# One more resident key-weight slice, a mixer ring of four single slices, and a new instruction order in an attention-and-mixer kernel

## Chip, cores and metric

The kernel runs on one core of one Trainium2 chip. The metric is the device time of one execution in microseconds; three executions of the kernel before gave 3256.13, 3258.33 and 3261.33 us, median 3258.33 us.

## What is computed

The reference applies four layers to 2048 tokens of width 640, attention (A), mixer (B), A, B, each with a residual and a layer norm ahead of it:

```python
x = x + _A_ref(_layernorm(x), A_mem0, A_Wq, A_Wk, A_Wv, A_Wo, A_seg_len)
x = x + _B_ref(_layernorm(x), B_w1, B_w2, B_w3, B_w4)
x = x + _A_ref(_layernorm(x), A_mem0, A_Wq, A_Wk, A_Wv, A_Wo, A_seg_len)
x = x + _B_ref(_layernorm(x), B_w1, B_w2, B_w3, B_w4)
```

Attention goes over 64 segments of 32 tokens, one after another. Each segment sees 8 memory tokens and itself (40 rows, 32 heads of 192), and the attention output of the memory tokens is the memory of the next segment:

```python
for s in range(n_seg):
    h = concatenate([mem, x[s*32:(s+1)*32]])      # 40 x 640
    q, k, v = h @ Wq, h @ Wk, h @ Wv              # 32 heads x 192
    o = (softmax(mask(q @ k.T * scale)) @ v) @ Wo # 40 x 640
    mem, out[s] = o[:8], o[8:]
```

The mixer is `h = gelu(layernorm(x) @ w1)`, a shift of its four channel quarters by -1, +1, -2 and +2 tokens, `x1 = x + h @ w2`, and `x1 + gelu(layernorm(x1) @ w3) @ w4` (w1, w2 640x640, w3 640x1536, w4 1536x640).

## The kernel before

**Steps and lanes.** The two attention layers run together: in step t (0 to 68, `attention_step(t)`) lane 0 works on segment t of the first layer and lane 1 on segment t-5 of the second. Steps 5 to 63 have both lanes, 80 rows; the first five and the last five have one, 40 rows. The two mixers run as one stream too: `chunk(c)` and `chunk_end(c)` work on 64 tokens of each lane (128 rows), one chunk in every two steps, spread between the attention work. Two steps and one chunk make a period of the trace. The last chunk runs by itself at the end.

**Attention in a step.** The 32 heads are 8 groups of 4, in 4 pairs `pr`. For a group TensorE makes keys `psk` and queries `psq` (`keys_queries`, 30 matmuls of 80 columns each, L928), values `psv` for the pair (L984, in tiles of 32 columns of the array), scores `pss` (L1044), the transposed weights `pst` (L1079), the output `pso` (L1096) and its share of the output projection `psy` (L1122, 30 matmuls in two halves). ScalarE copies qT, V, PT and oT out of PSUM (L939, L964, L1087, L1104) and does the exponential (L1063); VectorE copies kT and does the softmax. When the last `psy` of a step is done, VectorE copies the memory rows into `hT` (`fm`, L1149 for two lanes), for which the next step's keys and queries wait, and the token rows into `yTB` (`fy`, L1163 and L1165), for which the mixer's `psx` transposes (L1305) wait. In odd steps `fy` is four copies, in even steps two.

**Chunk.** psx, sum with the loaded residual `xw` (L1310), layer norm, transposes `psv` (L1202), w1 (`psh`, L1409), gelu, w2 (`hs`, L1468), layer norm, w3 (`psh`, L1531), gelu, w4 (`y`, L1577), L1592, a layer norm for the second attention, and `psn` (L1631), whose columns go into `hT` (`fc`, L1639). GpSimd's queue issues the loads of the next chunk: `lnx` (L1263) and four of `xw` (L1285). `psvl` (L1202 too) transposes the 64 rows of `lnx` for the first lane.

**Weights.** wq, wk and wv have five slices of 128 rows for a pair (1536 columns, 384 KB each). `STREAM[kind][pr]` of the five are loaded anew through the ring `wst` of twelve slots (`RING_A`, `load_pair`, L802), the rest stay on chip, and so does all of Wo. Odd steps take the pairs in reverse order, and the pair at the turn is kept, so that a step loads three pairs. The mixer's weights all stream, through the ring `wstB` of `RING_B` slots (`load_b`, L838 to L844). All these loads are issued on SyncE's queue in one order, each when its slot is free.

**The order.** Nothing runs in the order of the Python loops. `Plan.add` records every operation with a cost and its reads and writes; `Plan.place` then picks, engine by engine, the operation that its cost model lets start first, and among those within a few hundredths of a microsecond the one with the smallest rank. The ranks are the table `RANK`, a list for each kind of step and operation, found by a search. `OVER`, `DMA_RATE` and `RATE_ONE` belong to that cost model alone. What is built is a fixed order on each engine.

Of the kernel before, what the change touches and what calls it, by code (L numbers as in the profile page):

```python
# [22 lines left out]
STREAM = {"k": (4, 2, 2, 4), "q": (4, 2, 2, 4), "v": (4, 1, 1, 4)}  # L23
RING_A = 12
RING_B = 3
# [24 lines left out]
OVER = 0.0  # L50
PE_LAT = 0.22
DMA_RATE = 335.0e3
# [9 lines left out]
RATE_ONE = 350.0e3  # L62
# [6 lines left out]
        "apply_ln.f": (60.13, 185.694, 121.216, 72.37,),  # L69
        "chunk.f1": (175.755,),  # L70
        "chunk.f2": (76.908,),
        "chunk.f3": (157.464,),
        "chunk.fe": (133.631,),
        "chunk.fe3": (57.268,),
        "chunk.fel": (-12.647,),
        "chunk.fhr": (260.219,),
        "chunk.fhs": (203.515,),
        "chunk.fk0": (74.518,),
        "chunk.fk1": (194.333,),
        "chunk.fs": (103.426, 110.915,),  # L80
        "chunk.ft": (113.011,),
        "chunk.fw": (65.202, 75.684, 108.832, -50.712, 68.19, 10.815, 60.434, 122.265, 56.172, 161.413, 66.001,
            107.816, 153.37,),
        "chunk.fx": (114.535,),
        "chunk.fx0": (91.411, 111.515,),
        "chunk.fxu": (116.315,),
        "chunk.fz": (93.811,),
        "gelu.f1": (189.103, 112.842, 128.034, 132.117, 44.407, 147.123, 98.279,),
        "gelu.f2": (57.845, 81.849, 107.377, 125.496, 54.573, 170.821, 64.393,),
        "gelu.f3": (117.836, 38.035, 94.857, -4.703, 136.729, -25.232, 93.978,),  # L90
        "gelu.f4": (131.7, 41.437, 170.141, 69.53, 69.266, 116.495, 116.698,),
        "ln_ops.f1": (145.801, 200.678,),
        "ln_ops.f2": (71.886, 106.684,),
        "load_b.fn": (147.751, 23.09, 11.08, 11.355, 89.609, 6.762, 92.508, -1.573, 25.172, 111.488, 53.734,
            83.446, 82.888,),
        "transposes.f": (144.968, 58.96, 214.456,),
    },
    "chunk_end": {
        "apply_ln.f": (211.991,),
        "chunk_end.fc": (-27.709, 120.014, 238.626,),  # L100
        "chunk_end.fs": (74.033, 110.691,),
        "chunk_end.fst": (180.769, 113.382,),
        "chunk_end.ft4": (102.714,),
        "chunk_end.fw": (28.061, 167.286, 30.445, 89.214, 81.834, 168.442,),
        "chunk_loads.f": (195.767, 161.598, 81.116, 106.457, 112.814,),
        "chunk_loads.fz": (93.808,),
        "ln_ops.f1": (-34.553,),
        "ln_ops.f2": (106.46,),
        "load_b.fn": (135.743, 100.041, 78.2, 137.787, 32.979, 148.786,),
    },  # L110
    "first": {
        "attention_step.attend.f1": (148.378, 77.62, 114.96, 182.798, 67.707, 132.292, 117.437, 9.556,),
        "attention_step.attend.f2": (94.114, 45.338, 97.34, 2.921, 39.889, 158.104, 102.968, 120.888,),
        "attention_step.attend.f3": (111.391, 103.267, 58.209, 67.757, 59.663, 202.755, 84.112, 126.69,),
        "attention_step.attend.f4": (60.398, 144.455, 13.144, 68.985, 167.013, 76.809, 77.99, 116.342,),
        "attention_step.attend.f5": (165.673, 98.282, 108.051, -30.162, 100.241, 108.627, 50.844, 33.286,),
        "attention_step.attend.f6": (82.907, 61.972, 169.833, 50.782, 87.105, 1.277, 38.193, 13.451,),
        "attention_step.attend.f7": (57.571, 73.411, 92.596, 149.164, 43.781, 166.64, 114.181, 193.617,),
        "attention_step.attend.fs": (94.666, 40.135, 103.519, 45.088, 93.624, 126.408, 53.08, 100.642,),
        "attention_step.fm": (97.138,),  # L120
        "attention_step.fy": (152.471,),
        "attention_step.keys_queries.fk": (108.26, 63.879, 60.273, 80.616, 125.72, 79.278, 129.38, 120.256,),
        "attention_step.keys_queries.fk2": (73.153, 105.038, 173.824, 72.993, 110.733, 23.631, 43.071, 110.049,
            69.986, 59.459, 28.577, 130.679, 2.806, 21.99, 16.502, 38.137,),
        "attention_step.keys_queries.fn": (114.737, 87.54, 90.747, 134.363, 51.243, 12.969, 113.46, 18.309, 28.745,
            52.697, 18.142, 37.915, 100.944, 59.855, 136.199, 114.18, 5.659, 167.958, 120.015, 126.184, -8.685,
            81.081, 81.602, 179.073, 87.637, 106.4, 41.064, -12.77, -26.244, 87.387, 121.946, 65.385, 94.824,
            70.71, 51.535, 27.115, 114.677, 136.151, 54.568, 202.357, 1.163, 126.959, 46.11, 79.263, 50.203,
            103.218, 100.572, 28.338, 116.712, 119.833, 137.44, 106.323, 40.974, 87.854, 51.428, 27.582, 75.954,
            87.949, 63.925, 144.876, 25.025, 136.202, 11.073, 134.566,),  # L130
        "attention_step.keys_queries.fq": (124.433, 100.638, 54.881, 107.011, 54.88, 102.016, 85.177, 108.598,),
        "attention_step.project.f8": (-74.442, -42.266, 137.911, 68.456, 95.985, -20.623, -3.681, 126.264, 137.783,
            79.153, 124.656, 99.94, 174.748, 132.771, 48.335, -27.114,),
        "attention_step.v_copy.fe": (131.77, 40.6, 126.632, 26.958, 166.274, 137.131, 88.073, 100.927, 57.888,
            78.872, 57.842, 101.781, 163.971, 21.423, 65.236, 108.635,),
        "attention_step.values.fv": (121.916, 134.278, 159.944, 48.99, -37.717, 64.118, 22.938, -51.977,),
        "load_pair.fn": (152.205, 115.609, 58.339, 140.914, 17.015, 111.511, 22.712, 203.377, 25.175, 202.14,
            41.521, 59.495, 52.779, 169.347, 9.285, 112.577, 41.187, -43.215, 79.871, 114.893, 5.785, -25.152,
            70.491, 117.135, 22.224, 40.345, -6.819, 171.235, 20.723, -5.808, 154.45, 146.744, 99.11, 126.651,),
        "res_tile.fn": (-37.803, 60.152, -8.701, 68.506, -2.387, 95.473, 16.955, -87.282, 167.605, 123.352, -17.98,  # L140
            5.54, 86.376, 90.625, 112.221, 91.761, -108.652, 143.475, 62.803, 138.743,),
    },
    "last": {
        "apply_ln.f": (152.793, 163.662, 74.991,),
        "chunk.fc2": (46.568, 157.158,),
        "chunk.fhr": (84.809,),
        "chunk.fs": (125.199, 55.502,),
        "chunk.ft": (134.777,),
        "chunk.fw": (141.993, 98.819, 86.347, -34.206, 180.428, 155.267, 138.674, 27.312, 81.939, 168.933, 109.433,),
        "chunk.fx": (47.573,),  # L150
        "chunk.fxu": (60.041,),
        "chunk.fz0": (255.003,),
        "chunk.halves.fa": (88.067, 111.942, 48.413, 110.73,),
        "chunk.halves.fn": (100.468, 138.108,),
        "gelu.f1": (101.778, 153.798, 120.238, 107.304, 104.078, 95.762,),
        "gelu.f2": (88.059, 54.923, 64.114, 67.676, 143.026, 71.513,),
        "gelu.f3": (147.997, 245.442, 214.387, 69.54, 186.357, 71.876,),
        "gelu.f4": (177.876, 105.904, 39.072, 140.832, 33.224, 81.409,),
        "ln_ops.f1": (61.467, -50.049,),
        "ln_ops.f2": (110.805, 201.056,),  # L160
        "load_b.fn": (97.929, 101.637, 88.373, 99.2, 6.248, -22.885, 93.276, 79.47, 154.946, 116.487, 54.257,
            111.859, 111.308,),
        "transposes.f": (29.26, -72.55,),
        "warm.fwarm": (228.987, 45.787, 114.595, -52.726, 202.36, 124.17, 102.55, 80.655, 222.205, 89.395, 108.587,
            48.077, 96.179,),
    },
    "last_end": {
        "chunk_end.fs": (44.631, 85.191,),
        "chunk_end.fst": (110.886, 86.277, 2.303, 125.225,),
        "chunk_end.fw": (70.696, 6.036, 95.78, 131.599, -11.939, 104.166, 94.79, 51.751,),  # L170
        "load_b.fn": (0.449, 34.393, 103.284, 139.892, 157.41, 27.939,),
    },
    "start": {
        "apply_ln.f": (58.226,),
        "chunk_loads.f": (176.973, 88.206, 110.091,),
        "ln_ops.f1": (88.7,),
        "ln_ops.f2": (121.638,),
        "start.f1": (19.368,),
        "start.f2": (83.017,),
        "start.f3": (89.709,),  # L180
        "start.f4": (41.06,),
        "start.f5": (107.925, -3.163, 55.808, 83.534,),
        "transposes.f": (149.113,),
    },
    "step0": {
# [399 lines left out]
def kernel(  # L585
# [177 lines left out]
    def mm_us(n, m=128, k=1):  # L763
        return k * (max(54, n) / 2400.0 + 0.0025)
# [972 lines left out]
```

## Time and profile before

| | |
|---|---|
| median of three runs | 3258.33 us |
| the profiled execution: time, span | 3268.68 us, 3266.9 us |
| granted TensorE clock, mean | 0.993 |
| TensorE busy | 3149.0 us, 96% |
| VectorE, ScalarE, GpSimd busy | 70%, 57%, 8% |
| bytes moved | 833.44 MB, 255 GB/s |
| mixer loads `wstB` | 495 of 320 KB, 132 of 160 KB |
| attention loads `wst` | 556 keys, 556 queries, 418 values, 384 KB each |

The trace has one row for each instruction of an engine with its start and length, and names what ended an engine's idle time ahead of it. A matmul row runs from its issue to its result, some 0.2 us, while the next one can be issued after some 0.036 us (80 columns), so matmuls overlap in the trace. Therefore a pause of TensorE is best read from the starts of its groups, and the idle time that the trace gives is shorter than the pause.

### The profile page before, as it was taken

Reading aid. Unit: us, or ns where it says so; the run is one execution under the profiler, and the core shown is the slowest. Engines: PE = TensorE matmul, PEld = TensorE weight load, DVE = VectorE, ACT = ScalarE, POOL = GpSimd, SP = SyncE. Lnnn points to the kernel's source line nnn. Section 1 sums busy time; section 2 is a strip of 40 time slices with the busy share of each in tenths; the row PEclk is TensorE's granted clock in tenths of the full one; section 3 lists DMA queues with packets and bytes.
Section 4 is the critical chain, followed back from the end, with each engine's and each line's share of the span. In section 5 each row is a group of like instructions: output and inputs, shape, how many; then the busy total and the mean of one; then the engine's idle time right before and its main releaser. Section 6 shows DMA issues by size and latency. Waiting matters only on the chain.

```text
span 3266.9 us, 172868 instructions
## 1 busy us (share of the span) xinstructions
PE 3149.0 (96%) x77161; PEld 2790.2 (85%) x77161; DVE 2285.5 (70%) x7377; ACT 1854.6 (57%) x4217; POOL 269.6 (8%) x510
## 2 busy tenths in 40 slices
PE   5899999999999999999999999999999999999997
PEld 4778888888888888888888888888888888888875
DVE  3566777777677777777777777777777777767665
ACT  2345565666556666656565666565656665556443
POOL 0000000000000000000000000000000000000000
PEclk8999999999999999999999999999999999999999
DMA  9787777778777877787777777777877787778885
GB/s 372 264 286 236 237 265 253 241 235 273 246 237 249 280 239 234 253 272 239 245 262 258 241 237 269 253 241 244 281 247 238 244 274 249 238 244 277 275 277 199
DMA packets 409714, 833.44 MB, mean 255 GB/s; under 512 B 39651, under 2 KB 207280, under 8 KB 408969
## 3 DMA queue, kind: packets, MB, share of 16 engines
q1 hardware_dynamic: 401704, 809.47, 73.2%
q0 software_dynamic: 7104, 12.84, 1.3%
q8 instruction: 604, 9.90, 1.2%
q14 instruction: 142, 1.16, 0.1%
q10 hardware_dynamic: 160, 0.08, 0.0%
HBM read 816.98 MB, written 5.24 MB: 252 GB/s over the span
## 4 chain that ended last, share of the span: by engine, by line
PE 88%; DMA 7%; issue 2%; DVE 2%; ACT 1%; SPq 0%; POOL 0%; POOLq 0%; ACTq 0%; DVEq 0%
PE psq L928 16%; PE psy L1122 16%; PE psk L928 16%; PE psv L984 15%; PE pss L1044 5%; PE pso L1096 5%; PE psh L1531 3%; DMA wst<-in_A_Wq_dram 3%; PE y L1577 3%; PE pst L1079 2%; DMA wst<-in_A_Wk_dram 2%; PE psv L1024 2%; PE psh L1409 1%; PE hs L1468 1%; DMA wst<-in_A_Wv_dram 1%
## 5 line engine op out<-in xcount | busy, mean ns | idle before, releaser
L928 PEld LDWEIGHTS <-wst 128*128 128x128 bf16 x19872 | 803.7, 99 | 64.1 <-issue 35.7
L1122 PE MATMUL psy<-oT,wo 128*128 128x80 bf16 (+1 forms) x16560 | 703.6, 200 | 26.4 <-issue 8.6
L964 ACT CAST V<-psv 96x384 bf16<-96x384 f32 (+3 forms) x1264 | 595.9, 474 | 168.3 <-PE psv L984 102.4
L1122 PEld LDWEIGHTS <-wo 128*128 128x128 bf16 x16560 | 630.8, 99 | 51.2 <-issue 35.1
L928 PE MATMUL psq<-hT,wst 128*128 128x80 bf16 (+1 forms) x9936 | 518.0, 200 | 13.7 <-DMA wst<-in_A_Wq_dram 8.6
L928 PE MATMUL psk<-hT,wst 128*128 128x80 bf16 (+1 forms) x9936 | 508.6, 200 | 17.7 <-DVE hT L1149 9.6
L939 ACT CAST qT<-psq 128x480 bf16<-128x480 f32 (+1 forms) x552 | 291.8, 529 | 371.2 <-PE psq L928 352.0
L1104 ACT CAST oT<-pso 128x480 bf16<-128x480 f32 (+1 forms) x552 | 293.7, 532 | 264.0 <-PE pso L1096 238.9
L954 DVE CAST kT<-psk 64x160 bf16<-64x160 f32 (+1 forms) x1104 | 340.4, 308 | 131.3 <-PE psk L928 62.6
L984 PEld LDWEIGHTS <-hT 128*32 128x32 bf16 (+1 forms) x11840 | 295.5, 96 | 157.0 <-issue 5.2
L1063 ACT ACTIVATE Pm<-pss,sm 80x320 bf16<-80x320 f32 (+2 forms) x552 | 279.3, 506 | 195.9 <-DVE sm L1056 105.2
L1056 DVE CUSTOM_DVE_ANT_1 pss<-pss,mask 80x320 f32<-80x320 f32 (+2 forms) x552 | 257.1, 466 | 150.1 <-PE pss L1044 138.3
L1087 ACT COPY PT<-pst 80x320 bf16<-80x320 bf16 (+2 forms) x552 | 221.7, 402 | 239.2 <-PE pst L1079 233.3
L984 PE MATMUL psv<-wst,hT 128*32 128x384 bf16 (+1 forms) x5920 | 343.3, 326 | 2.2 <-issue 1.1
L984 PE MATMUL psv<-wv,hT 128*32 128x384 bf16 x5920 | 344.7, 328 | 0.5 <-issue 0.5
L1067 DVE TENSOR_REDUCE sm<-Pm 80x4 f32<-80x320 bf16 (+2 forms) x552 | 250.5, 454 | 109.6 <-ACT Pm L1063 98.1
L928 PE MATMUL psq<-hT,wq 128*128 128x80 bf16 (+1 forms) x6624 | 321.1, 200 | 4.1 <-DMA wq<-in_A_Wq_dram 2.7
L928 PE MATMUL psk<-hT,wk 128*128 128x80 bf16 (+1 forms) x6624 | 321.0, 200 | 3.4 <-issue 2.0
L928 PEld LDWEIGHTS <-wk 128*128 128x128 bf16 x6624 | 270.8, 99 | 17.6 <-issue 13.9
L947 DVE CAST kT<-psk 128x320 bf16<-128x320 f32 (+1 forms) x552 | 253.8, 460 | 45.6 <-PE psk L928 33.5
L1069 DVE TENSOR_TENSOR Pm<-Pm,sm 80x320 bf16<-80x320 bf16 (+2 forms) x552 | 256.2, 464 | 34.9 <-DVE sm L1068 0.9
L928 PEld LDWEIGHTS <-wq 128*128 128x128 bf16 x6624 | 267.4, 99 | 6.5 <-DMA wq<-in_A_Wq_dram 3.0
(131 smaller groups left out, 3777.6 us busy)
## 6 DMA issues: line engine op xcount, KB each, us to landing
wst<-in_A_Wk_dram SPq DMA_DIRECT2D x556, 384.0 KB, 4.9
wst<-in_A_Wq_dram SPq DMA_DIRECT2D x556, 384.0 KB, 5.0
wst<-in_A_Wv_dram SPq DMA_DIRECT2D x418, 384.0 KB, 5.1
wstB<-in_B_w_dram SPq DMA_DIRECT2D x495, 320.0 KB, 4.7
wstB<-in_B_w_dram SPq DMA_DIRECT2D x132, 160.0 KB, 4.3
wo<-in_A_Wo_dram SPq DMA_DIRECT2D x8, 960.0 KB, 12.3
wv<-in_A_Wv_dram SPq DMA_DIRECT2D x2, 1536.0 KB
xw<-in_A_x_dram POOLq DMA_DIRECT2D x32, 77.5 KB, 5.3
```

The costliest lines, as they stand in the source:

```text
L928: nc.tensor.matmul(out=o[:, cc, 0:W], lhsT=wv(kc, GW * j + cc * P, GW * j + (cc + 1) * P), rhs=h[:, kc, cw:cw + W], start=begin(pq), stop= ...
L939: nc.scalar.copy(out=qT[:, :, c0:c0 + N], in_=T(pq)[:, :, off:off + N])
L947: nc.vector.tensor_copy(out=k4[:, :, 0::3, c0:c0 + N], in_=p4[:, :, 0::2, off:off + N])
L954: copy(out=k4[r0:r1, :, jj, c0:c0 + N], in_=p4[r0:r1, :, 1, off:off + N])
L964: (nc.vector.tensor_copy if e == "DVE" else nc.scalar.copy)(out=v_part(*dst), in_=a_)
L984: nc.tensor.matmul(out=o[32 * u:32 * u + n3, :], lhsT=left[:, kc, 32 * g3:32 * g3 + n3], rhs=wv(kc, a, a + GWH), start=(kc == 0), stop=(kc ...
L1056: nc.vector.tensor_tensor_reduce(out=o, in0=o, in1=maskt.unsqueeze(1).to_broadcast([NR, HG, N]), scale=-scale, scalar=3.0e38, op0=ALU.add, ...
L1063: nc.scalar.activation(out=Pb[0:NR, :, 0:N], in_=o, func=ACT.Exp, bias=sm_[0:NR, 0:1], scale=-1.0)
L1067: nc.vector.tensor_reduce(out=sm_[0:NR, 2:2 + HG], in_=Pb[0:NR, :, 0:N], axis=AX.X, op=ALU.add)
L1069: nc.vector.tensor_tensor(out=Pb[0:NR, :, 0:N], in0=Pb[0:NR, :, 0:N], in1=sm_[0:NR, 6:6 + HG].unsqueeze(2).to_broadcast([NR, HG, N]), op=A ...
L1104: nc.scalar.copy(out=o_[:, :, off:off + N], in_=T(pso)[:, :, 0:N])
L1122: nc.tensor.matmul(out=o[:, m, cw:cw + W], lhsT=wo[:, cc, m * P:(m + 1) * P], rhs=o_[:, cc, 0:W], start=st, stop=True, skip_group_check=True)
```

## The change

Pair 1 of the keys keeps four of its five slices on chip instead of three. The mixer's ring becomes four slots of one slice (160 KB) instead of three slots of two (320 KB), so that its w1, w2, w4 and most w3 loads are of one slice and so are the matmul groups that use them; the last columns of w3 keep loads of two slices, which are 256 columns wide there. The last chunk keeps its loads as they were. A new `order` entry holds w1's matmuls behind the `psvl` transposes. The model's three constants are changed, and all of `RANK` is replaced by a new table. No arithmetic is changed, and the number of matmuls on TensorE is the same, 77161.

```diff
-STREAM = {"k": (4, 2, 2, 4), "q": (4, 2, 2, 4), "v": (4, 1, 1, 4)}
+STREAM = {"k": (4, 1, 2, 4), "q": (4, 2, 2, 4), "v": (4, 1, 1, 4)}
-RING_B = 3
+RING_B = 4
-OVER = 0.0
+OVER = 0.03
-DMA_RATE = 335.0e3
+DMA_RATE = 330.0e3
-RATE_ONE = 350.0e3
+RATE_ONE = 345.0e3
 RANK = {
-    ...
+    ...
 }
+    ONES = tuple((k, k + 1) for k in range(KC))
+    PAIRS = ((0, 2), (2, 4), (4, KC))
...
-            b.make = lambda: wring.tile([P, SLOT if last else 2 * Dm], bf16, name="wst" if last else "wstB",
+            b.make = lambda: wring.tile([P, SLOT if last else Dm], bf16, name="wst" if last else "wstB",
...
-            transposes(psl2, vx, TOK, D(0.11), (vxk,))
+            o_l = transposes(psl2, vx, TOK, D(0.11), (vxk,))
...
-        for i, (a, e) in enumerate(((0, 2), (2, 4), (4, KC))):
-            due = D(0.2 + 0.05 * i)
+        for i, (a, e) in enumerate(PAIRS if last else ONES):
+            due = D(0.2 + 0.05 * (a // 2) + 0.01 * (a % 2))
...
-            add("PE", mm_us(128, k=KC * (e - a)), due, fw, r=(wb, vTk, B("vTl"), B("vTd"), B("vTn", 0), B("vTn", 3)), a=tuple(pz))
+            add("PE", mm_us(128, k=KC * (e - a)), due, fw, r=(wb, vTk, B("vTl"), B("vTd"), B("vTn", 0), B("vTn", 3)), a=tuple(pz),
+                order=(o_l,) if ahead else ())
...
-        for i, (a, e) in enumerate(((0, 2), (2, 4), (4, 5))):
+        for i, (a, e) in enumerate(PAIRS if last else ONES):
...
-        for third, (n0, n1, units) in enumerate(((0, 5, ((0, 2), (2, 4), (4, KC))), (5, 10, ((0, 2), (2, 4), (4, KC))),
-                                                 (10, FC, ((0, KC),)))):
+        for third, (n0, n1, units) in enumerate(((0, 5, PAIRS if last else ONES), (5, 10, PAIRS if last else ONES),
+                                                 (10, FC, ((0, KC),) if last else PAIRS))):
...
-        for i in range(6):
-            a, e = 2 * i, 2 * i + 2
-            due = D(1.3 + 0.06 * i)
+        n4 = 2 if last else 1
+        for a in range(0, FC, n4):
+            e = a + n4
+            due = D(1.3 + 0.03 * a)
```

## The prediction

> **What bounds the kernel now.** First the page's busy line and its chain of work that ended last, then the busy time by stretches, which covers the start, the two-lane part and the end.
>
> ```profile
> PE 3149.0 (96%) x77161; PEld 2790.2 (85%) x77161; DVE 2285.5 (70%) x7377; ACT 1854.6 (57%) x4217; POOL 269.6 (8%) x510
> ...
> PE 88%; DMA 7%; issue 2%; DVE 2%; ACT 1%; SPq 0%; POOL 0%; POOLq 0%; ACTq 0%; DVEq 0%
> ```
> ```profile
> 100.00:300.00 200.00, 184.72 (x4822) 158.01 (x4819) 129.12 (x442) 92.94 (x250) 14.13 (x26) 1.00 0.79 268
> 300.00:3000.00 2700.00, 2668.09 (x65194) 2384.74 (x65194) 1961.80 (x6250) 1631.33 (x3615) 228.05 (x424) 1.00 0.75 250
> ```
>
> TensorE is the bound. Of 2700 us with two lanes it idles 31.9, and its 77161 matmuls stay. So the change is worth what it does to TensorE's pauses. TensorE's own waits say what ends them:
>
> ```profile
> PE psk L928 <- DVE hT L1149: 9.6, 29, 0.3
> PE psq L928 <- DMA wst<-in_A_Wq_dram: 8.6, 16, 1.1
> PE psk L928 <- DMA wst<-in_A_Wk_dram: 2.4, 6, 0.8
> ```
>
> The first comes 29 times, once per two steps. Idle time is counted from a matmul's result, 0.2 us after its issue, so pauses are longer than this; I read them from starts. This is the end of an odd step, TensorE and VectorE:
>
> ```profile
> 1525.85 0.31 PE L1079 MATMUL pst<-ident,Pm 80*128 80x80 bf16 x4
> 1526.12 0.70 PE L1122 MATMUL psy<-oT,wo 128*128 128x80 bf16 x15
> 1526.73 0.45 PE L1096 MATMUL pso<-PT,V 80*128 80x80 bf16 x8
> 1527.01 2.05 PE L1122 MATMUL psy<-oT,wo 128*128 128x80 bf16 x45
> 1529.39 0.81 PE L928 MATMUL psk<-hT,wst 128*128 128x80 bf16 x18 [0.33 <-DVE hT L1149]
> ```
> ```profile
> 1529.10 0.24 DVE L1149 CAST hT<-psy 128x80 bf16<-128x80 f32 x1 [3.83 <-PE psy L1122]
> 1529.25 0.33 DVE L1163 CAST yTB<-psy 128x150 bf16<-128x150 f32 x1
> 1529.47 0.17 DVE L1165 CAST yTB<-psy 128x10 bf16<-128x10 f32 x1
> 1529.55 0.32 DVE L1163 CAST yTB<-psy 128x150 bf16<-128x150 f32 x1
> 1529.77 0.17 DVE L1165 CAST yTB<-psy 128x10 bf16<-128x10 f32 x1
> ```
>
> From 1525.85 to 1529.39 are 3.54 us. Issued are 72 matmuls at 0.036 us (the pitch inside such groups), 2.59 us. Paused: 0.95. The last psy issues until about 1528.90 (result at 1529.06, less 0.2, plus its pitch), so 0.49 go to the wait for hT and 0.46 to psy waiting for oT and pso for PT. At an even step's end pst starts at 1575.09 and psk at 1578.70; issued there are 57 matmuls at 0.036 and 25 psh at 0.056, 3.45 us: 0.16 paused. Together 1.11 us in a period of 93.8.
>
> **The change, part by part.** Orders are read from the two built programs; all durations are from the trace.
>
> *Step ends.* From the issue end of pst to its pso the trace needs 0.73 us (1525.99 to 1526.73, with PT's copy of 0.42 between); from pso to its own psy 0.81 (1527.02, oT's copy from 1527.21 for 0.56, then 0.05). Before, 15 psy matmuls (0.54) stood in those places. In the new order 30 do (1.07), at odd and even ends: both waits go, 0.46 + 0.16 = 0.62 us per period.
>
> But at the steps' ends of the two-lane part VectorE now does fy (the yTB copies) ahead of fm (the hT copy), and at odd ends TensorE has psn and psx between the last psy and the first psk. psx needs all of fy. Counted from the last psy's issue: VectorE starts at 0.20; by the starts above the copies follow at 0.22, 0.08 and 0.22, the last takes 0.17, so fy ends at 0.89; psx starts at 0.94 (0.05 from copy to matmul, as 1529.34 to 1529.39) and takes 5 x 0.056 until 1.22. hT, behind fy, is ready at 0.80 + 0.24 + 0.05 = 1.09, earlier. psn (0.15) lies in between; its two copies of 0.29 and 0.17 end near 0.8. So psk starts at 1.22, of which 0.43 is work: a pause of 0.79 against 0.49, 0.30 us more. At even ends hT is ready at 0.20 + 2 x 0.29 + 0.24 + 0.05 = 1.07; the 20 psh matmuls now there hide 1.12 (before, ten hid the 0.49). With that cover gone it would cost up to 1.07 per period, 31 us. Net: 0.62 - 0.30 = 0.32 us gained, times 29 periods: **-9.3 us**.
>
> *psvl.* The five transposes psvl use 64 rows of the array instead of 128, and pauses of 0.1 us set them off on both sides (the pso ahead of them is issued by 1538.98):
>
> ```profile
> 1539.08 0.32 PE L1202 MATMUL psvl<-ident,vbg 64*128 64x64 bf16 x5
> 1539.33 0.82 PE L928 MATMUL psq<-hT,wq 128*128 128x80 bf16 x18
> ```
>
> Five at 0.029 end at 1539.23, psq starts at 1539.33. In the new order the values' psv follow psvl at once, and their own pause ahead of them, of the same size, is paid anyway: 0.1 x 29 = **-2.9 us**. The runs of psv otherwise number much the same (279 and 282).
>
> *The resident slice* takes one 384 KB load out of each step, about 68 x 0.39 = 27 MB, 3% of 833. It can save at most the waits of psq, psk and psv for wst, 8.6 + 2.4 + 0.8 = 11.8 us, and nothing where the slice was hidden anyway. With 0.75 busy DMA engines I take the low end, **-1 us**.
>
> *The ring.* More SyncE issues (35 instead of 19 per chunk, less one k slice a step), no bytes more. Landing times by size:
>
> ```profile
> wstB<-in_B_w_dram SPq DMA_DIRECT2D x495, 320.0 KB, 4.7
> wstB<-in_B_w_dram SPq DMA_DIRECT2D x132, 160.0 KB, 4.3
> ```
>
> The new risk is that a slot must be refilled between its use and the use four units on. Counted in matmul time along the orders, the shortest such distance was 7.6 us with three double slots; now it is 5.1, then 5.2, 5.7, 5.7, 5.9 and 6.1. A refill needs the landing and about 0.3 us from the last matmul's issue to the DMA's. With 4.3 that is 4.6: hidden. With a need of 5.4 it costs 0.3 + 0.2 per period, 15 us. Queued behind such a load on SyncE are the key, query and value slices. Nothing excludes a small gain, since the finer matmul groups can start on half the bytes; its bound is the 1.0 us that y waits for wstB. I take **+2 us**, near the median row; bounds -1 and +15.
>
> A page of the Trainium skill speaks against it. "DMA: Bandwidth & Descriptors", section "Measured (HBM→SBUF, 128 partitions, SWDGE, issued from GpSimd)", says to batch loads to 1 MiB or more, and its section "Anatomy of one DMA" fits a fixed 2 us plus bytes over 436 GB/s. By that fit a 160 KB load would take an estimated 2.4 us and sixteen more loads per chunk 32 us of fixed time if nothing overlapped, 930 us over 29 periods; the rows above, 0.4 us for half the size with loads overlapping, make me expect none of it.
>
> *The chunk's loads.* GpSimd's loads of xw (L1285) wait for the end of w4, which in the new order stands about 7.1 us ahead of the odd end instead of 16.6. After w4, 1.3 us pass until the first issue (L1592 twice, then 0.3), and four issues at 0.55 put the last at -4.15. Landing, by all tiles xw:
>
> ```profile
> DMA to landing us min/median/max: 2.0/4.9/7.1
> ```
>
> At the median it lands at +0.75, and the sum L1310 wants it at 1.22 + 0.24 = 1.46. VectorE is in order: kT copies and the layer norm for psv (L1202) stand behind L1310, the latter with nearly no slack. At the maximum every time it would cost 1.5 x 29 = 43 us. I take **+1 us**.
>
> *Ends of the kernel.* The one-lane steps are reordered too; TensorE idles 15.3 us from 100 to 300. The same covers counted there come out some longer, some shorter: 0, bounds 6 each way (ten steps at 0.6, a two-lane period's gain). The finer matmul groups cost nothing by themselves: inside and between groups the pitch is 0.036.
>
> **Sum.** -9.3 - 2.9 - 1 + 2 + 1 = -10.2 us. The profiled execution took 3268.68 us for a span of 3266.9, 0.3% over the median of 3258.33; so I take the sum off the median: **3248 us**. A measurement can tell 0.2%, 6.5 us, from no change.
>
> **Rivals.** (1) *The ring of four decides* (slower). Place: TensorE at the w3 and w4 units with 5.1 to 5.7 us of distance. Against: y waited only 1.0 us before. For: that was with 7.6 us; now there is 0.5 of slack over the median. If the need is 5.6, it costs 0.5 + 0.4 = 0.9 per period, 26 us: 3274. It outweighs the gain from a need of about 5.35. 0.18. (2) *xw lands late, or fy ahead of hT costs more than counted* (slower): 0.6 us per period more, 17 us: 3265. 0.10. (3) *Given back* elsewhere, by VectorE and ScalarE copies that now come in tighter places: 3255 to 3262. For: 70% VectorE. 0.22. (4) *Weight waits go too*: 10 us more, 3238. Against: 3% fewer bytes. 0.10. That the slice itself does nothing is part of my forecast, which lives on the order.
>
> **Numbers.** The forecast has 0.40, rival 4 0.10: faster 0.50; same 0.22; slower 0.28. The forecast's own range is 3238 to 3252. Below, -10 for weight waits and -6 for the ends with another few: 3226. Above, +15 for the ring, +10 for xw and +6: 3280, which takes in rival 1.
>
> **What would show it.** Right: in the trace after, hT starts about 0.64 us after the odd end's last psy result instead of 0.04, psk starts behind psx, pso and psy stop waiting for PT and oT, and psvl runs into psv. Wrong: waits of psh, hs or y for wstB of several tens of us; VectorE waiting at L1310 for xw; or a pause at even ends behind psh.

## The result and the profile after

The changed kernel took **3285.12 us** (median of six runs, 3270.94 to 3295.52) beside 3259.83 for the kernel before on the same chip: ratio 1.0075, 95% interval 1.0060 to 1.0089. It is slower by 20 to 29 us, under 1%; the forecast was 3248 with a range up to 3280. A second set of five runs gave 3279.84 and 1.0058 (1.0038 to 1.0078).

The executions in the two profiles understate this. Before's took 3268.68, far up in its spread, and after's 3270.94, the lowest of its six. So a second profile of each kernel, from the experiments, stands beside them below. Line numbers of after are those of before plus 4, from about L1410 on plus 5 or 6.

The page of after, busy line and chain of waits that ended last:

```profile
PE 3138.7 (96%) x77159; PEld 2781.0 (85%) x77161; DVE 2271.9 (69%) x7377; ACT 1861.6 (57%) x4217; POOL 267.1 (8%) x510
...
PE 86%; DMA 8%; issue 2%; DVE 2%; ACT 1%; SPq 1%; POOL 0%; DVEq 0%; POOLq 0%; ACTq 0%
```

TensorE is still the bound, with the same matmuls. Its share of the chain has gone from 88 to 86%, and DMA's and SyncE's queue (SPq) from 7 and 0 to 8 and 1. The stretch with two lanes (us, busy time of PE, PEld, DVE, ACT and POOL, clock, DMA share, GB/s):

```profile
300.00:3000.00 2700.00, 2658.48 (x65245) 2376.70 (x65242) 1952.87 (x6254) 1640.67 (x3617) 225.81 (x424) 1.00 0.73 242
```

The clock is at 1.00 as before and the DMA engines are less loaded, 0.73 instead of 0.75, since the resident slice took 27 MB away. TensorE nevertheless idles 41.5 us of these 2700 instead of 31.9. Its waits (us in total, times, longest):

```profile
PE psq L932 <- DMA wst<-in_A_Wq_dram: 20.1, 35, 1.3
PE psx L1309 <- DVE yTB L1169: 19.5, 31, 0.6
...
PE psk L932 <- DVE hT L1158: 1.7, 6, 0.3
```

The wait of psk for hT (9.6 us before) is gone and psx for yTB has come, as worked out. What was not: psq now waits 20.1 us for query slices where it waited 8.6. The end of the odd step that answers to the one shown of before, TensorE and then VectorE:

```profile
1519.93 0.45 PE L1100 MATMUL pso<-PT,V 80*128 80x80 bf16 x8
1520.22 2.32 PE L1126 MATMUL psy<-oT,wo 128*128 128x80 bf16 x60
1522.38 0.31 PE L1637 MATMUL psn<-ident,h2u 128*128 128x64 bf16 x5
1523.33 0.45 PE L1309 MATMUL psx<-ident,yTB 128*128 128x128 bf16 x5 [0.65 <-DVE yTB L1169]
1523.62 0.38 PE L932 MATMUL psk<-hT,wst 128*128 128x80 bf16 x6
```
```profile
1522.58 0.33 DVE L1167 CAST yTB<-psy 128x150 bf16<-128x150 f32 x1 [1.54 <-PE psy L1126]
1522.81 0.17 DVE L1169 CAST yTB<-psy 128x10 bf16<-128x10 f32 x1
1522.88 0.32 DVE L1167 CAST yTB<-psy 128x150 bf16<-128x150 f32 x1
1523.11 0.17 DVE L1169 CAST yTB<-psy 128x10 bf16<-128x10 f32 x1
1523.18 0.23 DVE L1153 CAST hT<-psy 128x80 bf16<-128x80 f32 x1
```

Thirty psy stand behind each pst and none waits. The last psy result is at 1522.54 and hT starts at 1523.18, 0.64 us later, the number of the prediction; psk comes right behind psx.

To see where the time went I added up TensorE's pauses from its starts (distance to the next matmul, less the pitch of its shape; pauses under some 0.06 us are left out) in steps 5 to 63, by what ended each. Columns are profiled executions; us, with the number of pauses. The last row is the time from the first psk of step 5 to the last psy of step 63, between which all five hold the same psk, psq and psy matmuls:

| ended by | before, again | after | after, again | two passed | one passed |
|---|---|---|---|---|---|
| wst (attention slices) | 6.8 x21 | 24.8 x56 | 32.0 x56 | 3.4 x8 | 10.2 x25 |
| wstB (mixer slices) | 0.3 x2 | 1.6 x10 | 1.1 x4 | 27.6 x52 | 2.4 x9 |
| PT and oT | 19.0 x116 | 1.1 x2 | 1.4 x3 | 1.1 x2 | 1.4 x3 |
| hT or psx (step ends) | 14.8 x30 | 23.9 x30 | 23.8 x30 | 23.8 x30 | 23.9 x30 |
| nothing shown, under 0.4 us | 9.6 x77 | 1.4 x8 | 3.1 x17 | 1.8 x9 | 2.1 x10 |
| nothing shown, longer | 10.2 x11 | 6.2 x9 | 4.7 x7 | 12.2 x14 | 10.6 x14 |
| other | 1.3 x6 | 9.9 x61 | 10.1 x62 | 9.6 x61 | 9.9 x62 |
| length of this part | 2773.9 | 2777.5 | 2781.1 | 2785.7 | 2767.6 |

(The last two columns are the runs in which query slices pass mixer loads, below.) The rows of PT and oT and of the step ends did what the sum said. The first row ate it.

### The profile page after: what moved, and what is told of

Read it like the earlier page. It is cut to its first block, busy times and chain, and to the rows that moved or that the text cites. A ratio compares the mean times of both kernels' runs of the same rounds, so it can differ in the third digit from the quotient of the medians.

```text
span 3269.2 us, 173866 instructions
## 1 busy us (share of the span) xinstructions
PE 3138.7 (96%) x77159; PEld 2781.0 (85%) x77161; DVE 2271.9 (69%) x7377; ACT 1861.6 (57%) x4217; POOL 267.1 (8%) x510
## 4 chain that ended last, share of the span: by engine, by line
PE 86%; DMA 8%; issue 2%; DVE 2%; ACT 1%; SPq 1%; POOL 0%; DVEq 0%; POOLq 0%; ACTq 0%
PE psy L1126 16%; PE psk L932 16%; PE psq L932 16%; PE psv L988 15%; DMA wst<-in_A_Wq_dram 6%; PE pso L1100 4%; PE pss L1048 4%; PE psh L1536 3%; PE y L1583 3%; PE pst L1083 2%; PE psv L1028 2%; PE psh L1413 2%; PE hs L1473 1%; PE psv L1206 1%; DMA wst<-in_A_Wk_dram 1%
## 5 line engine op out<-in xcount | busy, mean ns | idle before, releaser
L932 PEld LDWEIGHTS <-wst 128*128 128x128 bf16 x19044 | 777.4, 99 | 77.7 <-issue 37.6
L968 ACT CAST V<-psv 96x384 bf16<-96x384 f32 (+4 forms) x1264 | 589.9, 473 | 299.1 <-PE psv L988 207.2
L1126 PE MATMUL psy<-oT,wo 128*128 128x80 bf16 (+1 forms) x16560 | 692.9, 200 | 16.7 <-DMA wo<-in_A_Wo_dram 7.7
L932 PE MATMUL psq<-hT,wst 128*128 128x80 bf16 (+1 forms) x9936 | 529.9, 200 | 23.5 <-DMA wst<-in_A_Wq_dram 20.1
L932 PE MATMUL psk<-hT,wst 128*128 128x80 bf16 (+1 forms) x9108 | 493.0, 200 | 4.1 <-DVE hT L1158 1.5
L932 PE MATMUL psk<-hT,wk 128*128 128x80 bf16 (+1 forms) x7452 | 349.7, 200 | 3.9 <-issue 2.7
L988 PE MATMUL psv<-wv,hT 128*32 128x384 bf16 (+1 forms) x5920 | 344.8, 328 | 1.2 <-issue 1.1
L932 PEld LDWEIGHTS <-wk 128*128 128x128 bf16 x7452 | 301.0, 99 | 19.3 <-issue 14.6
```

The costliest lines, as they stand in the source:

```text
L932: nc.tensor.matmul(out=o[:, cc, 0:W], lhsT=wv(kc, GW * j + cc * P, GW * j + (cc + 1) * P), rhs=h[:, kc, cw:cw + W], start=begin(pq), stop= ...
L968: (nc.vector.tensor_copy if e == "DVE" else nc.scalar.copy)(out=v_part(*dst), in_=a_)
L988: nc.tensor.matmul(out=o[32 * u:32 * u + n3, :], lhsT=left[:, kc, 32 * g3:32 * g3 + n3], rhs=wv(kc, a, a + GWH), start=(kc == 0), stop=(kc ...
L1126: nc.tensor.matmul(out=o[:, m, cw:cw + W], lhsT=wo[:, cc, m * P:(m + 1) * P], rhs=o_[:, cc, 0:W], start=st, stop=True, skip_group_check=True)
```

## The experiments

The first four runs were expected under three theories that the first expectation defines: R (the ring), O (the order) and S (small loads).

**Theory Q** came after them, from the traces of after: SyncE issues its loads in order, and its mixer loads, mostly of 160 KB, cost it as much each as those of before, mostly of 320. Between 400 and 2900 us they took 206.3 us of issuing for 506 loads before and 383.7 for 932 after, 0.41 us each in both. And query slices now stand in its queue behind mixer loads: issued within 0.15 us of the load before them were 11 of 426 before and 102 of 425 after, and that load was a mixer load 7 and 83 times. Between 400 and 2900 us 18.0 of the 22.4 us that psk and psq waited for slices fell on slices so close behind a mixer load. **Rivals:** the ring of four is too short (rival 1 of the prediction); the new matmul order leaves the slices too late whatever SyncE does; the DMA engines serve finer loads worse.

One such wait in the trace of after, SyncE and TensorE:

```profile
1013.11 0.79 SPq L846 DMA_DIRECT2D wstB<-in_B_w_dram  x1
1013.94 0.43 SPq L806 DMA_DIRECT2D wst<-in_A_Wq_dram  x1
```
```profile
1018.59 0.38 PE L932 MATMUL psk<-hT,wst 128*128 128x80 bf16 x6
1019.79 0.39 PE L932 MATMUL psq<-hT,wst 128*128 128x80 bf16 x6 [0.82 <-DMA wst<-in_A_Wq_dram]
```

The slice goes out at 1013.94, right behind a mixer load that held SyncE for 0.79 us. Its first matmul could have started at about 1018.8, 4.9 us later, and the median landing of such slices is 4.9. There is no room for the 0.8.

**Changed kernel once more** (no edit).

> The changed kernel itself, for a second trace. Theory R (the ring): mixer loads wait on SyncE for one of only four single slots, and the query and key slices queued behind them come late; then the time is near 3285 us and TensorE's waits for wst and wstB are at least twice the 22 us that the first trace shows in its two-lane part. Theory O (the order): the new order calls streamed slices sooner after their issue, whatever the ring; the same trace is expected, waits for wst alone. Theory S (small loads): single-slice loads cost the DMA engines or SyncE more; landing times of wst above the 4.9 us of the first trace.

3279.84 us (3274.82 to 3281.41), 1.0058 (1.0038 to 1.0078). The loss is there again, with psq waiting 27.9 us 46 times in the profiled run.

**No pacing.**

```diff
-        elif o.paced:
+        elif False:
```

> The changed kernel without the extra dependence that holds a load's issue until a given TensorE group is done (the pace); loads are issued as soon as their slot is free, in the same order. Theory O in the form that the pace issues loads too late: falls by 15 us or more, below 3270, and the waits for wst mostly go. Theory R: slots, not the pace, hold the loads back: within 6 us of the changed kernel. Theory S: within 6 us or slower, as loads crowd.

3367.41 us, 1.0327 (1.0293 to 1.0361): far worse. Theories O and R had less or the same time, and S had allowed for more, as loads crowd; but the loss is in a row that no theory had. The waits of TensorE:

```profile
PE psq L932 <- issue: 25.8, 25, 2.4
PE psk L932 <- issue: 25.7, 26, 3.7
...
PE psq L932 <- DMA wst<-in_A_Wq_dram: 15.8, 24, 1.7
```

"Issue" is time in which the engine waited for nothing that the profile shows. Long pauses of this kind grew from 6.2 us to 69.2, while those for wst were 17.8 (24.8 and 32.0 in the two profiles of after). What they wait for is taken up in the last section. Key slices took 6.4 us to land instead of 4.9.

**Ring of six single slots, same order.**

```diff
+    for o in placed:
+        for b in o.slots:
+            if o.dma and b.cls == "rb":
+                b.slot = len(loads_b) % 6
+                loads_b.append(b)
```

> The changed kernel in the same order on every engine, its mixer loads dealt to six single slots instead of four. Room for them comes from leaving out the fourth resident key slice of pair 1: its matmuls read the third one's weights, so 384 KB less are loaded once, at the start. Theory R: the distance from use to refill grows by half, and the time falls by 15 to 25 us to 3260 to 3270. Theory O and theory S: within 6 us of the changed kernel, 3279 to 3291.

3279.73 us (3270.14 to 3282.61), 1.0055 (1.0038 to 1.0072): the same as after. Two more slots remove nothing; pauses for wst are 25.6 us. The depth of the ring is not the cause, and rival 1 falls. The loads keep their order on SyncE in this run.

**Kernel before, each double mixer load as two single ones** into the same slot.

```diff
-                nc.sync.dma_start(out=v, in_=w4_v[:, a:e, :])
+                for i in range(n):
+                    nc.sync.dma_start(out=v[:, i:i + 1], in_=w4_v[:, a + i:a + i + 1, :])
```

> The kernel before with every mixer load of two slices (320 KB) issued as two loads of one slice into the two halves of the same slot; ring, order and everything else as before. Theory S: slower by 10 to 25 us, 3270 to 3285. Theory R and theory O: within 6 us of 3259.

3270.06 us (ten runs), 1.0031 (1.0017 to 1.0045). Finer loads alone cost about 10 us (6 to 15), as theory S had it, with no change in order, bytes or slots. Pauses for wst stay at 6.1 us there, so it is not the same loss:

```profile
PE psq L933 <- DMA wst<-in_A_Wq_dram: 6.7, 15, 0.8
```

This bears on theory Q. SyncE's mixer loads take 417 us of issuing between 400 and 2900 us here, more than in after, yet only 27 of 426 query slices follow a mixer load within 0.15 us, and the time from a query slice's issue to its first matmul is that of before (5.5 us at the lower tenth). So more issues alone make no slice late; what this order lacks is query slices that stand directly behind mixer loads. Where the 10 us lie I could not find: no row of the table moves by more than 4, and in the profiled run the steps up to 4, the two-lane part and the end are longer by 3.6, 4.2 and 6.2 us.

**Kernel before once more** (no edit), for a typical profile.

> The kernel before once more, for the profile of a typical run (the one shown took 3268.68 us, 8 over the median of the 17 other runs). Every theory expects a time equal to before's, ratio 1.000, and in the trace: query slices issued back to back behind a mixer load on SyncE in about 12 of 426 cases, matmuls waiting for wst about 12 us in all.

3262.62 us, 0.9994 (0.9979 to 1.0010); the profiled run took 3258.63 and gave the table's first column. Two of 427 query slices follow a mixer load within 0.15 us, and psq waits less for them than in the first profile:

```profile
PE psq L928 <- DMA wst<-in_A_Wq_dram: 4.5, 10, 0.7
```

**Every streamed slice passes the mixer loads.** Each attention load is put ahead of up to two mixer loads in front of it on SyncE, where its slot is free by then.

```diff
+    for o in [o for o in placed if own(o, "ra")]:
...
+        if j < i:
+            o.start = min(o.start, placed[j].start)
+            placed.insert(j, placed.pop(i))
```

> The changed kernel, but where a load of a key, query or value slice stands on SyncE directly behind one or two mixer loads it is put ahead of them (same loads, same matmul order). Theory Q (SyncE's queue: sixteen more issues per chunk at 0.41 us each put query slices behind mixer loads, 102 of 425 instead of 11, and 18 of the 22.4 us of waits for weights in the trace of after are for such slices): these waits fall to about 4 to 6 us, time 3260 to 3264. Rival R (the loads land later because the finer transfers use the DMA engines worse): the waits stay at 20 us or more and the time stays at 3280. Rival M (the mixer loads, now later, are waited for instead): waits for wstB rise by 10 us or more and the time stays at 3275 to 3285.

3892.15 us, 1.1941 (1.1899 to 1.1983). This was my mistake: several slices in a row pass the same mixer load, which so slides back far more than one place. The trace still says something: pauses for wst fall to 3.1 us, and those for wstB rise to 446. Its waits:

```profile
PE y L1583 <- DMA wstB<-in_B_w_dram: 141.0, 64, 4.5
PE psh L1536 <- DMA wstB<-in_B_w_dram: 136.5, 35, 5.3
```

**hT copied ahead of yTB, psx behind 24 matmuls of psk and psq.**

```diff
+        if y is not None:                       # y: fy's place, o: fm
+            placed.insert(y, placed.pop(i))
...
+        placed.insert(j, placed.pop(i))         # psx, then its sum xw
```

> The changed kernel, but at the steps' ends VectorE copies hT (fm) ahead of yTB (fy), and psx with its sum xw stands behind 24 matmuls of psk and psq. By my step sum the pause at an odd end falls from 0.79 us to 0.34, 0.45 x 29 = 13 us: 3267. A rival says that what is saved at the end is given back as a longer wait for query slices a microsecond or two later, since the loads are released by matmuls: then 3275 to 3280, with the pauses at the end gone and the waits for wst up by about 10 us.

3297.59 us, 1.0104 (1.0078 to 1.0131), by the ratios 10 to 15 us worse than after, so both expectations missed. The pause at the step end fell only from 23.9 to 17.8 us, because ScalarE's copy of psn was next late, and the psv transposes a few microseconds on began to wait:

```profile
PE psv L1206 <- ACT qT L943: 17.6, 28, 0.6
PE psk L932 <- ACT hT L1645: 13.1, 29, 0.5
```

The profile names qT for the first line. These transposes read vbg, which comes out of the sum xw that I had moved back: it starts 1.94 us after the last psy result here (1539.92) and 1.28 in after (1523.82). So that chain may be the real one; this was not tried apart. The row "other" rose to 36.8 us. The waits for slices stayed (26.8), so the given-back theory finds no support either.

**Both edits together.**

> Both of these edits together: query slices ahead of mixer loads on SyncE, and hT copied ahead of yTB. If the two costs are separate they add: 3280 - 18 - 13 = 3249, which would be 10 us under the kernel before. If one feeds the other, 3260.

3902.6 us, 1.1957 (1.1913 to 1.2000): the slice edit's mistake covers everything, and nothing follows on whether the two add.

**Only query slices pass, up to two mixer loads**, each mixer load passed at most once.

```diff
+    for o in [o for o in placed if getattr(o.fn, "kind", 0) == "q"]:
...
+        j, left = i, 2
```

> The changed kernel, but in each period only the few query slices that stand on SyncE directly behind a mixer load pass it (one or two mixer loads, each passed at most once), instead of every streamed slice as in the run before. Theory Q (SyncE's 0.41 us per issue makes these slices late): the waits of psq for wst fall from 20 to 28 us to about 10, and if the delayed mixer loads have room the time is 3265 to 3270. Rival M (the mixer loads have no room in a ring of four single slices, so an issue later means a wait): waits for wstB rise by as much as the others fall, time 3275 to 3285. In the run that moved every slice, waits for wst fell to 3 us and waits for wstB rose to 446.

3277.6 us, 1.0044 (1.0027 to 1.0060). Rival M holds: pauses for wst fall from 24.8 and 32.0 us to 3.4, pauses for wstB rise from 1.6 and 1.1 to 27.6. Its waits:

```profile
PE y L1584 <- DMA wstB<-in_B_w_dram: 10.7, 20, 0.9
...
PE psh L1537 <- DMA wstB<-in_B_w_dram: 7.3, 15, 1.0
```

That names the resource: one place in SyncE's queue, which two loads want. But it is uneven. By place in the period (77 loads in the same order in each of 23 periods), the mixer load directly in front of a query slice had 3.8, 6.9 and 8.6 us between landing and use after it was passed (medians, at the three places where slices were late); the one in front of that had 0.05 in both cases in which a second was passed.

**Double loads in after's order**: a ring of three slots of 320 KB.

```diff
+        b.slot = ndbl % 3
+        b.make = lambda b=b: wring.tile([P, 2 * Dm], bf16, name="wstB", tag=f"rb{b.slot}")
...
+            o.fn = fn2                          # loads both slices
+            placed.remove(o2)
```

> The changed kernel with its matmul order, but the mixer slices loaded in pairs again into a ring of three double slots, one load of 320 KB where there were two of 160 KB (w3's last third stays in three loads). The room comes from one resident key slice of pair 1 whose place another slice is read from, so the output of that part is not the reference's; loads and matmuls are as many. This undoes the ring alone. Theory Q: SyncE issues 21 instead of 35 mixer loads per chunk, query slices stand less often behind them, waits of psq fall to about 8 us and the time falls by 15 to 20 us to about 3260. Rival O (the new matmul order itself leaves the query slices too late, whatever the ring): waits of psq stay at 20 us or more, time 3272 to 3280.

3420.09 us, 1.0471 (1.0446 to 1.0496). It doesn't undo the ring alone: a pair is loaded at its first slice's place, the three single loads of w3's last third each take a whole slot, and SyncE is then held longer at w3 with the key slices behind it:

```profile
PE psk L934 <- DMA wst<-in_A_Wk_dram: 91.0, 48, 3.4
PE psx L1311 <- DVE yTB L1171: 19.5, 31, 0.6
```

In the two-lane part 73 us of pauses fall on key slices issued behind a mixer load. It shows again what a load held on SyncE does to those behind it, but as a test of the ring it is void.

**Earlier pacing.**

```diff
-PACE = 0.25
+PACE = -0.6
```

> The changed kernel with PACE at -0.6 instead of 0.25: every paced load is released about 0.85 us of matmul work earlier, nothing else moves. If the late slices are held by the pacing, their lead rises from 5.0 to 5.8 us, waits for wst fall below 10 us and the time falls to about 3265. If they are held by SyncE's own queue or by a slot that is not free yet, waits for wst stay at 20 us or more and the time at 3275 to 3285; more loads in flight at once may add some waits for instructions, of which the run without any pacing had 69 us.

3293.66 us, 1.0092 (1.0073 to 1.0111). Pauses for wst do fall, to 15.7 us, and long pauses in which nothing is shown rise from 6.2 to 25.5, a third of the way to the run without pacing. So the slices can be had sooner by an earlier release, but not for free.

**Query slices pass exactly one mixer load**, at four places in a period (the edit beside that of the run with two).

```diff
-        j, left = i, 2
+        j, left = i, 1
```

> The changed kernel, but a query slice that stands on SyncE directly behind a mixer load passes exactly that one load (four places in a period). In the run before, where two could be passed, the load passed at each of these places had 3.8 us or more to spare afterwards, and it was the second one passed (once in w3, once in w4) whose median spare time fell to 0.05 us. Theory Q (SyncE's queue makes the slices late): waits of psq for wst fall from 20 to 28 us to about 10, waits for wstB stay under 5 us, time 3260 to 3266, close to the kernel before. Rival M (whatever goes second on SyncE is late, the sum of both waits stays): sum at 25 us or more, time 3277.

**3260.36 us** (12 runs, 3252.82 to 3271.6), **0.9998 (0.9984 to 1.0013)**: the whole loss is gone with one place on SyncE, at the same matmul order and ring. The slice that moves also takes over the release time of the load that it passes, so place and release have moved together. Pauses for wst are 10.2 us, for wstB 2.4. The page's chain and the waits:

```profile
PE 88%; DMA 6%; issue 2%; DVE 2%; ACT 1%; SPq 0%; POOL 0%; DVEq 0%; POOLq 0%; ACTq 0%
```
```profile
PE psx L1310 <- DVE yTB L1170: 19.5, 31, 0.6
PE psq L933 <- DMA wst<-in_A_Wq_dram: 10.8, 21, 2.2
```

The chain has its 88% TensorE back. The two slices go out together, the mixer load behind them:

```profile
1016.05 1.41 SPq L806 DMA_DIRECT2D wst<-in_A_Wq_dram  x2
1017.50 0.43 SPq L847 DMA_DIRECT2D wstB<-in_B_w_dram  x1
```

At the three places where slices were late in after (lead is issue to first matmul, spare is landing to first matmul, medians in us; late means spare under 0.2; the trace has the landing in 17 of 23 periods):

| loads ahead, after | lead, spare, late in after | lead, spare, late with one passed |
|---|---|---|
| one w4 load, held by psh | 5.42, 0.08, 9 | 5.70, 1.01, 1 |
| a w3 and a w4 load | 5.36, 0.50, 5 | 5.64, 0.80, 1 |
| four w4 loads | 5.43, 0.05, 14 | 5.77, 0.40, 5 |

About 0.3 us more lead turns 28 late slices into 7. The query slice that follows the middle place pays a little, 9 late instead of 4.

**The same with six slots and earlier pacing of the mixer loads.**

```diff
-            while k >= 0 and done[k].end + PE_LAT > o.start + PACE:
+            while k >= 0 and done[k].end + PE_LAT > o.start + PACE - 1.5 * own(o, "rb"):
```

> The run before in this list (one mixer load passed), and the ring of six single slots, and the mixer loads' pacing 1.5 us earlier. One resident key slice of pair 1 is not kept, another is read in its place, so that part of the output is not the reference's. If the ring of four is what holds SyncE and makes the rest late, the waits for both kinds of slices fall to under 10 us together and the time to 3250 to 3258. If the order of the matmuls and the ring of twelve for the attention slices set it, nothing is gained over the run with the swap alone; earlier loads may cost waits for instructions, as in the runs with earlier or no pacing (26 and 69 us).

3256.98 us, 0.9991 (0.9978 to 1.0004). Pauses for both kinds of slices are 7.5 us together, as the room theory had it, but the interval covers the run with the swap alone: what room in the ring is worth beyond the swap can't be told from nothing.

**Kernel before, one streamed key slice less.**

```diff
+    placed = [o for o in placed if not getattr(o.fn, "skip", False)]
```

> The kernel before in its own order, with the first streamed key slice of pair 1 not loaded (its matmuls read the resident slice beside it, so that part of the output is not the reference's): one load of 384 KB fewer per step, as in the change, and nothing else. My sum had -1 us for this, with at most the 7 to 12 us that psq, psk and psv wait for weights: 3255 to 3264. A rival says that fewer bytes free the DMA engines and all loads land earlier: 3253 or less, with the waits for wst under 3 us.

3256.57 us (12 runs), 0.9985 (0.9973 to 0.9998). The missing load is worth about 5 us, 1 to 9, more than the 1 of my sum. Pauses for wst are 7.3 us against 6.8, so the rival, that all loads land earlier and the waits go, has no support in the trace, and neither has my reason for a gain. Where the 5 us lie is open.

## Why the prediction was wrong, by its steps

**Step ends: right.** PT and oT went from 19.0 us to 1.1 and 1.4, 0.61 us per period where 0.62 was worked out. The pause at the ends went from 14.8 to 23.9, 0.31 more per period where 0.30 was worked out; hT starts 0.64 us behind the last psy result. Net -8.7 for -9.3.

**psvl: right.** In after psv follows psvl at once:

```profile
1528.20 0.45 PE L1048 MATMUL pss<-kT,qT 128*128 128x80 bf16 x6
1528.59 0.32 PE L1206 MATMUL psvl<-ident,vbg 64*128 64x64 bf16 x5
1528.84 0.35 PE L988 MATMUL psv<-wv,hT 128*32 128x384 bf16 x4
```

The pause behind psvl, 0.093 us, came 28 times in the two-lane part: 2.6 us for the -2.9. The values' psv start 235 times with such a pause in before and in after, and in after the 28 behind psvl are among these; so one pause is saved per period. The table's row of short pauses falls by more, from 9.6 us to 1.4 and 3.1, but that isn't all gain: 28 of its 77 pauses stand ahead of psvl (0.098 us, 2.8 in all), and these are still there in after (some 0.10 us), where the profile names vbg and they count as "other".

**The resident slice: too small.** About -5 (-9 to -1) measured alone, for -1; what it is worth in the changed kernel no run shows. I bounded its use by the weight waits of before; that these could grow was not in the step.

**The ring: this step failed.** It says of SyncE only "More SyncE issues (35 instead of 19 per chunk, less one k slice a step), no bytes more", and prices the mixer's own landing. That term was right as far as it went: wstB was waited for 1.1 to 1.6 us, the bounds were -1 and +15. What it put at nothing is the wait of the attention slices that come to stand behind mixer loads, in a queue that is served in order at some 0.41 us an issue. Rival 1 has the sentence "Queued behind such a load on SyncE are the key, query and value slices", but I took it for a consequence of a late mixer load and looked for the wait at w3 and w4. No mixer load need be late: the slices behind them had a lead of 5.5 us at their lower tenth before (query slices), against a landing of 4.9, and after they have 5.2 there, with 84 of 425 under 5.5 instead of 24 of 426. I had read distances to the next use for the mixer's ring and for none of the others. The cost was 18 to 25 us of waits for wst, and moving these slices by one place took about 20 us off the whole. How much of it is due to the finer loads and how much to the new order is not shown: the finer loads in the old order bring none of these waits, and the new order with double loads was tried only in the void run.

**Two terms that were not in the sum.** The row "other" grew from 1.3 us to about 10. Of its 61 pauses 28 are those ahead of psvl, which are old; 29, 4.8 us in all, are new: pss in its new place directly behind pst, for which the profile names TensorE's own pst. That is a price of the order, but not by the copies of VectorE and ScalarE that rival 3 had in mind. And finer loads cost some 10 us by themselves in the kernel before, 462 loads more at 0.02 us each, which the prediction put at nothing. The Trainium skill, "DMA: Bandwidth & Descriptors", section "Measured (HBM→SBUF, 128 partitions, SWDGE, issued from GpSimd)", advises large loads, and its direction held. The fixed 2 us per load of its section "Anatomy of one DMA", which the prediction quotes for loads that don't overlap, is a hundred times what that run shows with loads that do.

**xw and VectorE: no cost.** VectorE waited at L1314 for xw once, 1.8 us; the median landing fell from 4.9 to 2.3:

```profile
DMA to landing us min/median/max: 1.6/2.3/5.7
```

**The tally** of the two second profiles: wst +25.2, wstB +0.8, PT and oT -17.6, ends +9.0, short pauses -6.5, long ones -5.5, other +8.8: +14.2. This part became 7.2 us longer, so about 7 us went the other way in distances that the table does not count. The spans (3256.9 and 3273.5) differ by 16.6: the rest lies ahead of step 5 (+6.1) and behind step 63 (+3.2) and is not explained; the two profiles of after differ ahead of step 5 by 6.2 among themselves. With one place swapped this part is 6.3 us shorter than before, and the whole comes out even with before: the version that follows from the experiments beats after, but not before.

## What to carry to other kernels

A load has two prices, its landing and its place in the queue that issues it. When a change makes loads finer or orders them anew, ask which loads come to stand directly behind others, what the issues ahead of them take by the trace, and how much lead they have over their landing; those with no lead to spare pay, not the ones that were split. The number of issues alone says little: the kernel before with split loads issues nearly as many and has none of these waits. Bounding a term by the waits of before holds only for what can shrink: a list of leads per load shows which of them can grow.

Where a load is late because of its place, look for a neighbour with time to spare before changing sizes or depths. A single swap with the load directly ahead, which had 3.8 to 8.6 us to spare, did what six slots and earlier release did not.

## What the runs showed of the hardware

Releasing loads earlier made TensorE pause for something that is not in its waits. Long pauses with nothing shown rose from 6.2 us to 25.5 with release 0.85 us earlier and to 69.2 with no pacing, although fewer bytes per microsecond were moved (247, 245 and 239 GB/s). The page of after lists the program itself among the DMA traffic:

```profile
q8 instruction: 605, 9.91, 1.2%
```

(packets, MB, share of the engines). The traces say that these pauses are waits for such packets. The packets have 16 KB each, and TensorE's 154852 instructions (matmuls and weight loads, with their semaphore waits) are 256 for each packet. Counted along these instructions, the long pauses with nothing shown between 300 and 3000 us, 66 without pacing, 28 with earlier release, 8 in after and 12 in before again, all stand at one place in a block of 256, give or take one instruction. The last packet to end before each of them is the same one by number, counted along with the blocks, and most of them end 1.3 to 1.6 us after it, where a point of time taken at random lies 0.5 to 5 us behind a packet. Why packets come late when weights are released earlier is not shown: no run takes either traffic away.

The issue of a mixer load on SyncE took 0.41 us on the mean in before, where most are of 320 KB, and in after, where most are of 160. Landing took 4.7 us for 320 KB in before; in after half the bytes took 0.7 us less:

```profile
wstB<-in_B_w_dram SPq DMA_DIRECT2D x1056, 160.0 KB, 4.0
wstB<-in_B_w_dram SPq DMA_DIRECT2D x66, 128.0 KB, 2.8
```
